# Decode attention with a gMLP branch: two heads interleaved over the partitions, 64 positions each

## The chip, the cores and the metric

The kernel runs on one core of one Trainium2 chip. The metric is the device time of one launch in microseconds (us), the median of several runs. A second source of numbers is one profiled execution of the same program, with a record of every instruction and every transfer.

## What is computed

One token `x` of 576 numbers is normalised to `xn`. Two branches read `xn`, and their results are added to `x`:

```python
# A: attention of 32 query heads over 16 key/value heads, head size 128,
#    over the last W = 4096 positions of the caches
q = (xn @ wq).reshape(32, 128)
k, v = k_cache[:, -4096:], v_cache[:, -4096:]      # each is used by two query heads
p = softmax(q @ k.T * 128 ** -0.5)
A = (p @ v).reshape(4096) @ wo                     # 4096 -> 576
# B: gMLP on one token
z = gelu(xn @ w_in)                                # 576 -> 4608
B = (z[:2304] * (w_sp * layernorm(z[2304:]) + b_sp)) @ w_out
out = x + A + B
```

All inputs and the output are bf16. Keys and values of one head are 1 MB each, so 32 MB of the 51 MB that are read are keys and values.

## The kernel before

**Loads.** All large inputs come through one queue, SP's, in a fixed order: `wq` in two pieces, the keys of the head pairs 0 and 1, `w_in` in three pieces, then in turn the keys of pair m and the values of pair m - 2 up to the last pair (7), the values of pairs 6 and 7, `w_out`, and `wo` in four pieces of 16, 10, 4 and 2 rows per partition. The pairs' loads are called k0 to k7 and v0 to v7 below. Each load fills one of seven slots of 20.7 KB per partition (pool `ring`); a load waits on SP until the slot it takes over has been read by its last user. `load_kv` puts position `32 p + t` of either head on partition p: two stretches of 8 KB per partition and load.

**Scores.** The loop over the 16 heads j works in groups of four (`GK = 4`, group g, place o = 0 to 3 in it). `t_head(j)` turns a head's keys with two 32x32 block transposes on VectorE (each 128x1024, as float32 pairs of bf16) into a tile `kT`; three such tiles exist. `s_head(j)` runs eight matmuls of 8 output rows and 512 columns: four accumulate (`be`) for either half `hf` of the positions. The result of head i of the group lies in rows 32 i to 32 i + 7 of the PSUM tile `S[g % 2]`, so a head uses one 32-column strip of the array. In a strip's eight rows, four rows `a` stand for four quarters of the partitions and two for the two query heads.

**Softmax of a group.** `sm_a(g)` takes the row maximum, lets `spread` exchange it between rows (two 32x32 transposes, a reduction, a copy), and ScalarE computes one exp over 128x1024 with the row sums into `lx`. `sm_b(g)` transposes the result `p` once (128x1024 bf16) into `pt`, runs `spread` again for the sums, takes the reciprocal `rs`, and ScalarE copies 16 pieces of 32x32 (as float32) from `pt` into `PT`, four per head.

**Values.** `pv(g)` runs 32 matmuls of 512 columns: 8 blocks `tb` of four positions, and in each block four heads i on four strips. `yb(g)` multiplies `ops` by `rs` and a mask (`om`), sums (`on`), and brings the result with 8 small matmuls into the columns of `Y`.

**Order.** The order of the instructions on each engine is the order in which the program writes them (`manual_schedule`). For head j of group g it is: `t_head(j)`; `sm_a(g - 1)` at o = 0 or `sm_b(g - 1)` at o = 1; `s_head(j)`; `yb(g - 2)` at o = 0; `pv(g - 1)` at o = 3. The gMLP's 162 matmuls (`z_mms`) come after head 3, its pointwise part (`z_rest`) after head 5 and `z_norm` after head 6. Behind the loop stand

```python
sm_a(3); sm_b(3); yb(2); pv(3); out_hv(0); out_hv(1); yb(3); out_hv(2)
for t, wv in wo_sb: out_mms(Y, t, wv, False, t == 31)
```

where `out_mms` runs four matmuls of 144 columns on four strips. The 128 matmuls of `wo` need all of `Y`, so also `yb(3)`. The heads' transposes are called t(0) to t(15) below, the score matmuls S(0) to S(15), and pv(g), exp(g), pt(g), om(g), Y(g) belong to group g.

Of the kernel before, what the change touches and what calls it, by code (L numbers as in the profile page):

```python
# [8 lines left out]
FP32 = mybir.dt.float32  # L9
BF16 = mybir.dt.bfloat16  # L10
ALU = mybir.AluOpType
ACT = mybir.ActivationFunctionType
AXX = mybir.AxisListType.X
# [3 lines left out]
HKV = 16  # L17
DH = 128
SK = 65536
W = 4096  # L20
F = 4608
FH = 2304
NT = W // 128
TB = 8
NB = NT // TB
GK = 4
NG = HKV // GK
NR = 98
NF = FH // 128
CW = D // 4  # L30
EPS = 1e-5
SCALE = DH ** -0.5
GELU_C = 0.7978845608028654
RING = 7
NS = 9
SLOT = NF * D
# [3 lines left out]
def kernel(  # L40
# [14 lines left out]
    nc = tc.nc  # L55
    P = nc.NUM_PARTITIONS

    const = ctx.enter_context(tc.tile_pool(name="const", bufs=1))
    work = ctx.enter_context(tc.tile_pool(name="work", bufs=2))
    ring = ctx.enter_context(tc.tile_pool(name="ring", bufs=RING))  # L60
    ktpool = ctx.enter_context(tc.tile_pool(name="ktpool", bufs=3))
    ps_s = ctx.enter_context(tc.tile_pool(name="ps_s", bufs=1, space=bass.MemoryType.PSUM))
    ps_o = ctx.enter_context(tc.tile_pool(name="ps_o", bufs=1, space=bass.MemoryType.PSUM))
    ps_m = ctx.enter_context(tc.tile_pool(name="ps_m", bufs=1, space=bass.MemoryType.PSUM))
    ps_a = ctx.enter_context(tc.tile_pool(name="ps_a", bufs=1, space=bass.MemoryType.PSUM))

    ctx.enter_context(tc.manual_schedule())

# [3 lines left out]
    def ring_tile(name, rows, width):  # L72
        t = ring.tile([P, SLOT], BF16, name=name, tag="ring")
        return t[:, 0:rows * width].rearrange("p (s c) -> p s c", c=width)
# [6 lines left out]
        return [(lo + s, v[:, s, :]) for s in range(n)]  # L81

    def load_kv(src, m, name):
        v = ring_tile(f"{name}{m}", 2, NT * DH)
        nc.sync.dma_start(v, src[0, 2 * m:2 * m + 2, SK - W:SK, :].rearrange("h (p t) d -> p h (t d)", p=P))
        return {2 * m + h: v[:, h, :].rearrange("p (t d) -> p t d", d=DH) for h in range(2)}

    def load_n(src, per, lo, n, name):
        v = ring_tile(f"{name}{lo}", n, D)
# [3 lines left out]
    K, V = {}, {}  # L93
    wq_sb = load_halves(A_wq, 0, 5, "wq") + load_halves(A_wq, 5, 4, "wq")
    for m in range(2):
        K.update(load_kv(A_k_cache, m, "k"))
    win_sb = sum((load_halves(B_w_in, lo, 3, "win") for lo in (0, 3, 6)), [])
    for m in range(2, HKV // 2):
        K.update(load_kv(A_k_cache, m, "k"))
        V.update(load_kv(A_v_cache, m - 2, "v"))  # L100
    for m in range(HKV // 2 - 2, HKV // 2):
        V.update(load_kv(A_v_cache, m, "v"))
    wout_sb = load_n(B_w_out, NF, 0, NF, "wout")
    wo_sb = []
    for n in (16, 10, 4, 2):
# [14 lines left out]
    ident = const.tile([P, P], BF16, name="ident")  # L120
# [18 lines left out]
    mask4 = const.tile([P, 4], FP32, name="mask4")  # L139
    nc.vector.reduce_sum(mask4[:], ident[:].rearrange("p (a x) -> p a x", a=4), axis=AXX)  # L140

    idv = ident[:].rearrange("p (i c h) -> p i c h", i=4, h=2)[:, :, 0:4, :]
    cm = const.tile([P, 4], FP32, name="cm")
    nc.vector.tensor_reduce(out=cm[:], in_=idv.rearrange("p i c h -> p c i h"), op=ALU.add,
                            axis=mybir.AxisListType.XY)
    dmask = const.tile([P, 4, DH], FP32, name="dmask")
    nc.gpsimd.tensor_copy(dmask[:], cm[:].unsqueeze(2).to_broadcast([P, 4, DH]))
    ihm = const.tile([P, 4, 2], FP32, name="ihm")
    nc.vector.reduce_sum(ihm[:], idv.rearrange("p i c h -> p i h c"), axis=AXX)

    sel = const.tile([P, 4, 32], FP32, name="sel")
    nc.gpsimd.memset(sel[:], 0.0)
    selv = sel[:].rearrange("p q (i h e) -> p q i h e", i=4, h=2)
    for dq in range(4):
        nc.gpsimd.tensor_copy(selv[:, dq, :, :, dq], ihm[:])
    S = []
    for n in range(2):
        t = ps_s.tile([P, 2, 512], FP32, name=f"S{n}")
        nc.vector.memset(t[:], 0.0)
        S.append(t)  # L160
    ops = ps_o.tile([P, 512], FP32, name="ops")
    nc.vector.memset(ops[:], 0.0)

    mx = const.tile([P, 32], FP32, name="mx")
    nc.gpsimd.memset(mx[:], 0.0)
    lx = const.tile([P, 32], FP32, name="lx")
    nc.gpsimd.memset(lx[:], 1.0)
    mb = const.tile([P, 32], FP32, name="mb")
    nc.gpsimd.memset(mb[:], 0.0)
    lb = const.tile([P, 32], FP32, name="lb")  # L170
    nc.gpsimd.memset(lb[:], 1.0)


    nc.tensor.matmul(ps_x[:, 0:NS], lhsT=rmat[:], rhs=x64[:], start=True, stop=True)  # L174
# [6 lines left out]
        out=junk[:], in0=x_col[:], in1=x_col[:], scale=1.0, scalar=0.0,  # L181
# [23 lines left out]
    for s, wv in wq_sb:  # L205
        for g in range(4):
            nc.tensor.matmul(  # L207
                qps[32 * g:32 * g + 2, :], lhsT=XT[:, s, :], rhs=wv[:, 512 * g:512 * (g + 1)],
                start=(s == 0), stop=(s == NS - 1), tile_position=(0, 32 * g),
# [12 lines left out]
    for k in range(4):  # L222
        for be in range(4):
            nc.tensor.matmul(
                qps2[:, k, be, :].rearrange("p (r g) -> p r g", r=2),
                lhsT=q_rep[0:NR, 2 * k + be // 2, be % 2].rearrange("p a d -> p (a d)"),
# [12 lines left out]
    KT = {}  # L239
    st = {}  # L240

    def t_head(j):
        kT = ktpool.tile([P, NT, 2, 32, 2], BF16, name=f"kT{j}", tag="kT")
        src = K[j].rearrange("p t d -> p (t d)").bitcast(FP32)
        dst = kT[:].rearrange("p t b k e -> p (t b k e)").bitcast(FP32)
        for hf in range(2):
            nc.vector.transpose(dst[:, 1024 * hf:1024 * (hf + 1)], src[:, 1024 * hf:1024 * (hf + 1)])  # L247
        KT[j] = kT

    def s_head(j):  # L250
        g, i = divmod(j, GK)
        kv = KT.pop(j)[:].rearrange("p t b k e -> p b e t k")
        for hf in range(2):
            for be in range(4):
                nc.tensor.matmul(  # L255
                    S[g % 2][32 * i:32 * i + 8, hf, :],
                    lhsT=Qb[:, j, be].rearrange("p a h -> p (a h)"),
                    rhs=kv[:, be // 2, be % 2, 16 * hf:16 * hf + 16, :],
                    start=(be == 0), stop=(be == 3), tile_position=(0, 32 * i),
                )  # L260

    def spread(col, buf, g, op, name):

        tr = work.tile([P, 32], FP32, name=f"{name}t{g}", tag=f"{name}t")
        nc.vector.transpose(tr[:], col[:])  # L265
        rd = work.tile([P, 2], FP32, name=f"{name}r{g}", tag=f"{name}r")
        nc.vector.tensor_reduce(out=rd[:], in_=tr[:, 0:8].rearrange("p (c h) -> p h c", h=2), op=op, axis=AXX)
        nc.vector.tensor_copy(buf[:, 0:8].rearrange("p (c h) -> p c h", h=2),
                              rd[:].unsqueeze(1).to_broadcast([P, 4, 2]))
        bk = work.tile([P, 32], FP32, name=f"{name}b{g}", tag=f"{name}b")  # L270
        nc.vector.transpose(bk[:], buf[:])  # L271
        return bk

    def sm_a(g):
        s = S[g % 2]
        nc.vector.tensor_reduce(out=mx[:, 0:1], in_=s[:], op=ALU.max, axis=mybir.AxisListType.XY)  # L276
        bk = spread(mx, mb, g, ALU.max, "m")
        nm = work.tile([P, 1], FP32, name=f"nm{g}", tag="nm")
        nc.vector.tensor_scalar_mul(nm[:], bk[:, 0:1], -SCALE)  # L279
        p = work.tile([P, 1024], BF16, name=f"p{g}", tag="p")  # L280
        nc.scalar.activation(p[:], s[:].rearrange("p a n -> p (a n)"), ACT.Exp, bias=nm[:, 0:1], scale=SCALE,  # L281
                             accum_out=lx[:, 0:1])
        st[g] = {"p": p}

    def sm_b(g):
        d = st[g]
        pt = work.tile([P, NT, 32], BF16, name=f"pt{g}", tag="pt")
        nc.vector.transpose(pt[:].rearrange("p t x -> p (t x)"), d["p"][:])  # L288
        lbk = spread(lx, lb, g, ALU.add, "l")
        rs = work.tile([P, 1], FP32, name=f"rs{g}", tag="rs")  # L290
        nc.vector.reciprocal(rs[:], lbk[:, 0:1])
        PT = work.tile([P, GK, NT, 2], BF16, name=f"PT{g}", tag="PT")
        pt4 = pt[:].rearrange("p t x -> p (t x)").bitcast(FP32).rearrange("p (t x) -> p t x", x=16)
        PT4 = PT[:].rearrange("p i t h -> p (i t h)").bitcast(FP32).rearrange("p (i t) -> p i t", i=GK)
        for i in range(GK):
            for a in range(4):
                nc.scalar.copy(PT4[32 * a:32 * a + 32, i, :], pt4[32 * i:32 * i + 32, :, a])  # L297
        d["PT"] = PT
        d["rs"] = rs

    def pv(g):
        d = st[g]
        for tb in range(NT // 4):
            for i in range(GK):
                nc.tensor.matmul(  # L305
                    ops[32 * i:32 * i + 8, :],
                    lhsT=d["PT"][:, i, 4 * tb:4 * tb + 4, :].rearrange("p t h -> p (t h)"),
                    rhs=V[GK * g + i][:, 4 * tb:4 * tb + 4, :],
                    start=(tb == 0), stop=(tb == NT // 4 - 1), tile_position=(0, 32 * i),
                )  # L310

    def yb(g):
# [64 lines left out]
        nc.vector.tensor_mul(hv[:], G[:, 0], zn[:])  # L377
        return hv

    for j in range(HKV):  # L380
        t_head(j)
        g, o = divmod(j, GK)
        if g > 0 and o == 0:
            sm_a(g - 1)
        if g > 0 and o == 1:
            sm_b(g - 1)
        s_head(j)
        if j == GK - 1:
            zps = z_mms()
        if j == GK + 1:  # L390
            G, sz = z_rest(zps)
            out_t = ps_a.tile([P, CW], FP32, name="out_t", tag="a")
            nc.vector.memset(out_t[:], 0.0)
        if j == GK + 2:
            hv = z_norm(G, sz)
        if g > 1 and o == 0:
            yb(g - 2)
        if g > 0 and o == 3:
            pv(g - 1)
# [58 lines left out]
```

## Time and profile before

| | before |
|---|---|
| median of 3 runs | 128.6 us (128.56 to 128.67) |
| the profiled execution: device time, span of its instructions | 128.68 us, 126.9 us |
| mean granted TensorE clock | 0.781 |
| busy: PE, VectorE (DVE), ScalarE (ACT), GpSimd (POOL) | 70.5, 74.1, 22.9, 3.6 us |
| read from memory | 50.96 MB, 402 GB/s over the span |
| transfers: packets of SP's queue, share of 16 engines' time | 5800, 95.2% |

Each line of groups names the source line, engine, operation, output and inputs, shapes and count, then the busy time and the mean duration of one instruction, then the engine's idle time just before it and what ended it. Matmuls are pipelined: a group's mean duration is a latency, and its rate is read from the times at which its matmuls start. "PEclk" is the granted TensorE clock, 1.00 being full speed.

### The profile page before, as it was taken

The page shows a single profiled execution, that of the slowest core. Times are in us where ns is not written, and L with a number is a line of the kernel's source. Part 1 is how long each engine was busy: PE and PEld are TensorE (multiplying, and loading weights), DVE is VectorE, ACT ScalarE, POOL GpSimd, SP SyncE. Part 2 cuts the span into 40 slices and gives each one's busy share as a digit, 9 for nine tenths or more (in the row PEclk, how much of TensorE's full clock was granted, in tenths as well). Part 3 has the DMA queues.
Part 4 walks back from the last instruction along what each step waited for, and adds up shares of the span by engine and source line. Part 5 has one row for each costly group of instructions (what it writes and reads, how often), then busy time and mean ns, then how long its engine had stood idle before and what let it go on. Part 6 is the DMA issues. An engine that isn't in the chain of part 4 may idle for free.

```text
span 126.9 us, 1775 instructions
## 1 busy us (share of the span) xinstructions
PE 70.5 (56%) x708; PEld 32.5 (26%) x708; DVE 74.1 (58%) x157; ACT 22.9 (18%) x76; POOL 3.6 (3%) x19
## 2 busy tenths in 40 slices
PE   0002831399999796008359456991579901862460
PEld 0002301132699621002113111231113301222350
DVE  6704145999000499455399799997999557050000
ACT  0300011000000003930000308303074039200000
POOL 3401000000000000000100000000000000000000
PEclk9999996579985559955868976999555996589755
DMA  4999999999999999999999999999999999999940
GB/s 136 433 409 429 408 429 434 444 436 418 427 413 431 418 426 429 421 431 434 421 436 423 424 436 423 429 424 421 429 431 423 431 452 442 427 418 413 415 171 0
DMA packets 5899, 51.06 MB, mean 402 GB/s; under 512 B 516, under 2 KB 516, under 8 KB 772
## 3 DMA queue, kind: packets, MB, share of 16 engines
q1 hardware_dynamic: 5800, 50.96, 95.2%
q8 instruction: 5, 0.08, 0.2%
q10 hardware_dynamic: 92, 0.00, 0.0%
q14 instruction: 2, 0.02, 0.0%
HBM read 50.96 MB, written 0.00 MB: 402 GB/s over the span
## 4 chain that ended last, share of the span: by engine, by line
issue 41%; DVE 27%; DMA 25%; PE 3%; POOLq 0%; POOL 0%
DMA wo<-in_A_wo_dram 18%; DVE kT L247 16%; DMA x<-in_A_x_dram 7%; PE out_t L403 2%; DVE mx L276 2%; DVE pt L288 2%; DVE on L319 2%; DVE om L315 1%; PE yps L322 1%; PE ps_x L184 0%; POOLq L453 0%; POOL mv L190 0%; DVE mt L265 0%; DVE lb L271 0%; DVE mb L271 0%
## 5 line engine op out<-in xcount | busy, mean ns | idle before, releaser
L255 PE MATMUL S<-kT,Qb 128*8 128x512 bf16 x128 | 40.5, 484 | 21.8 <-DVE kT L247 21.0
L247 DVE STREAM_TRANSPOSE kT<-k 128x1024 f32<-128x1024 f32 x32 | 37.0, 1211 | 10.8 <-DMA k<-in_A_k_cache_dram 10.8
L255 PEld LDWEIGHTS <-Qb 128*8 128x8 bf16 x128 | 11.7, 98 | 46.7 <-issue 38.5
L297 ACT COPY PT<-pt 32x32 f32<-32x32 f32 x64 | 15.4, 241 | 13.7 <-DVE pt L288 12.9
L281 ACT ACTIVATE p<-S,nm 128x1024 bf16<-128x1024 f32 x4 | 4.5, 1113 | 54.8 <-DVE nm L279 54.8
L305 PE MATMUL ops<-v,PT 128*8 128x512 bf16 x128 | 13.3, 453 | 0.4 <-ACT PT L297 0.4
L334 PEld LDWEIGHTS <-win 128*128 128x128 bf16 x162 | 10.1, 164 | 0.4 <-issue 0.4
L334 PE MATMUL zps<-XT,win 128*128 128x2 bf16 x162 | 10.2, 202 | 0.0
L322 PE MATMUL yps<-on,sel 128*32 128x32 f32 x32 | 2.1, 220 | 10.8 <-DVE on L319 10.8
L403 PE MATMUL out_t<-wo,Y 128*1 128x144 bf16 x128 | 3.7, 276 | 5.2 <-DMA wo<-in_A_wo_dram 5.2
L276 DVE TENSOR_REDUCE mx<-S 128x1 f32<-128x1024 f32 x4 | 4.8, 1204 | 1.6 <-PE S L255 1.6
L425 DVE TENSOR_TENSOR res<-out_t,x 97x144 bf16<-97x144 f32 x1 | 0.3, 308 | 9.1 <-PE out_t L403 9.1
L288 DVE STREAM_TRANSPOSE pt<-p 128x1024 bf16<-128x1024 bf16 x4 | 4.8, 1210 | 1.4 <-ACT p L281 1.4
L305 PEld LDWEIGHTS <-PT 128*8 128x8 bf16 x128 | 4.0, 91 | 5.8 <-issue 2.0
L174 PE MATMUL ps_x<-x,rmat 64*128 64x9 bf16 x1 | 0.2, 163 | 9.5 <-DMA x<-in_A_x_dram 9.5
L315 DVE SCALAR_TENSOR_TENSOR om<-ops,rs,dmask 128x512 f32<-128x512 f32 x4 | 3.0, 742 | 4.2 <-PE ops L305 4.2
L322 PEld LDWEIGHTS yps<-on,sel 128*32 128x32 f32 x32 | 1.7, 132 | 12.5 <-DVE on L319 10.4
L403 PEld LDWEIGHTS <-Y 128*1 128x1 bf16 x128 | 2.9, 97 | 6.0 <-issue 5.9
L207 PE MATMUL qps<-wq,XT 128*2 128x512 bf16 x36 | 3.8, 603 | 0.8 <-DVE XT L198 0.8
L319 DVE TENSOR_REDUCE on<-om 128x128 f32<-128x512 f32 x4 | 4.1, 1023 | 0.1
L218 DVE CAST q_rep<-qps 128x512 bf16<-128x512 f32 x2 | 1.4, 692 | 4.4 <-PE qps L207 3.7
L216 ACT CAST q_rep<-qps 128x512 bf16<-128x512 f32 x2 | 1.2, 585 | 14.2 <-DVE q_rep L218 14.2
(88 smaller groups left out, 35.0 us busy)
## 6 DMA issues: line engine op xcount, KB each, us to landing
k<-in_A_k_cache_dram SPq DMA_DIRECT2D x8, 2048.0 KB, 24.9
v<-in_A_v_cache_dram SPq DMA_DIRECT2D x8, 2048.0 KB, 21.7
win<-in_B_w_in_dram SPq DMA_DIRECT2D x3, 1728.0 KB, 20.6
wout<-in_B_w_out_dram SPq DMA_DIRECT2D x1, 2592.0 KB, 27.4
wq<-in_A_wq_dram SPq DMA_DIRECT2D x1, 2560.0 KB, 8.8
wo<-in_A_wo_dram SPq DMA_DIRECT2D x1, 2304.0 KB
wq<-in_A_wq_dram SPq DMA_DIRECT2D x1, 2048.0 KB, 13.0
wo<-in_A_wo_dram SPq DMA_DIRECT2D x1, 1440.0 KB
```

Of the source, the lines that this page charges most:

```text
L247: nc.vector.transpose(dst[:, 1024 * hf:1024 * (hf + 1)], src[:, 1024 * hf:1024 * (hf + 1)])
L255: nc.tensor.matmul(S[g % 2][32 * i:32 * i + 8, hf, :], lhsT=Qb[:, j, be].rearrange("p a h -> p (a h)"), rhs=kv[:, be // 2, be % 2, 16 * hf ...
L276: nc.vector.tensor_reduce(out=mx[:, 0:1], in_=s[:], op=ALU.max, axis=mybir.AxisListType.XY)
L281: nc.scalar.activation(p[:], s[:].rearrange("p a n -> p (a n)"), ACT.Exp, bias=nm[:, 0:1], scale=SCALE, accum_out=lx[:, 0:1])
L288: nc.vector.transpose(pt[:].rearrange("p t x -> p (t x)"), d["p"][:])
L297: nc.scalar.copy(PT4[32 * a:32 * a + 32, i, :], pt4[32 * i:32 * i + 32, :, a])
L305: nc.tensor.matmul(ops[32 * i:32 * i + 8, :], lhsT=d["PT"][:, i, 4 * tb:4 * tb + 4, :].rearrange("p t h -> p (t h)"), rhs=V[GK * g + i][:, ...
L315: nc.vector.scalar_tensor_tensor(out=om[:].rearrange("p c d -> p (c d)"), in0=ops[:], scalar=d["rs"][:, 0:1], in1=dmask[:].rearrange("p c ...
L319: nc.vector.reduce_sum(on[:], om[:].rearrange("p c d -> p d c"), axis=AXX)
L322: nc.tensor.matmul(yps[32 * g:32 * g + 32, :], lhsT=sel[:, dq, :], rhs=on[:, 32 * dq:32 * dq + 32], start=(dq == 0), stop=(dq == 3), tile_ ...
L334: nc.tensor.matmul(zps[:, :, t], lhsT=wt[:, t, :], rhs=XT[:, s, :], start=(s == 0 and t == 0), stop=(s == NS - 1 and t == NF - 1), skip_gr ...
L403: nc.tensor.matmul(out_t[32 * n:32 * n + 1, :], lhsT=lhs[:, col:col + 1], rhs=wv[:, CW * n:CW * (n + 1)], start=first, stop=last, tile_pos ...
```

## The change

Half-heads take the place of heads. A pair's keys (and values) now lie with head 0 on the even and head 1 on the odd partitions, 64 consecutive positions of 16 KB on each. One step of the loop (`t_half`, `s_half`) handles half of the 64 positions for both heads of a pair; there are still 16 steps, and four steps make a group of two pairs.

- `load_kv` asks for one stretch of 16 KB per partition. The order, the sizes and the slots of the loads stay.
- `t_half` transposes as much as `t_head` did. `s_half` runs eight matmuls, four for head 0 on strip `pr`, then four for head 1 on strip `2 + pr` (`pr` is the pair in the group). Each reads all of `kT`, every fourth bf16 of it instead of every second.
- exp is done by two instructions of 64 rows, one per head `hd`, into every second column of a tile `pz` of 128x2048 that GpSimd has set to zero at the start.
- `pt` becomes 128x2048: two transposes instead of one.
- The sums are spread by one float32 matmul with a constant matrix `lsum` (result `lps`), a maximum with 0.5 and a reciprocal, instead of `spread`.
- The 16 copies into `PT` are 32x64 instead of 32x32.
- `pv` still runs 32 matmuls of 512 columns, now with 16 output rows, in 16 blocks of two: only the strips 0 and 1 are used.
- The order of the tile pools in memory is changed (`lead`, then `ring` come first), and the constants `cm`, `sel` follow the new order of rows.

```diff
     def load_kv(src, m, name):
-        v = ring_tile(f"{name}{m}", 2, NT * DH)
-        nc.sync.dma_start(v, src[0, 2 * m:2 * m + 2, SK - W:SK, :].rearrange("h (p t) d -> p h (t d)", p=P))
+        t = ring.tile([P, SLOT], BF16, name=f"{name}{m}", tag="ring")
+        v = t[:, 0:TP * DH]
+        nc.sync.dma_start(v, src[0, 2 * m:2 * m + 2, SK - W:SK, :].rearrange("h (r t) d -> r h (t d)", t=TP))
...
+    lsum = const.tile([P, 4, 8, 2, 2], FP32, name="lsum")
+    nc.gpsimd.memset(lsum[:], 0.0)
...
+    for n in range(2):
+        t = const.tile([P, TP, 16, 2], BF16, name=f"pz{n}")
+        nc.gpsimd.memset(t[:], 0.0)
+        pz.append(t)
...
-    def s_head(j):
-        kv = KT.pop(j)[:].rearrange("p t b k e -> p b e t k")
-        for hf in range(2):
+    def s_half(m, hf):
+        kv = KT.pop((m, hf))[:].rearrange("p t b r x e -> p b e x t r")
+        for hd in range(2):
+            i = 2 * hd + pr
             for be in range(4):
                 nc.tensor.matmul(
                     S[g % 2][32 * i:32 * i + 8, hf, :],
-                    lhsT=Qb[:, j, be].rearrange("p a h -> p (a h)"),
-                    rhs=kv[:, be // 2, be % 2, 16 * hf:16 * hf + 16, :],
+                    lhsT=Qb[:, 2 * m + hd, be].rearrange("p a h -> p (a h)"),
+                    rhs=kv[:, be // 2, be % 2, hd],
...
-        nc.scalar.activation(p[:], s[:].rearrange("p a n -> p (a n)"), ACT.Exp, bias=nm[:, 0:1], scale=SCALE,
-                             accum_out=lx[:, 0:1])
+        for hd in range(2):
+            lo, hi = 64 * hd, 64 * hd + 64
+            nc.scalar.activation(p[lo:hi, :, :, hd], s[lo:hi].rearrange("p a (t r) -> p (a t) r", r=16), ACT.Exp,
+                                 bias=nm[lo:hi, 0:1], scale=SCALE, accum_out=lx[lo:hi, 0:1])
...
-        nc.vector.transpose(pt[:].rearrange("p t x -> p (t x)"), d["p"][:])
-        lbk = spread(lx, lb, g, ALU.add, "l")
-        nc.vector.reciprocal(rs[:], lbk[:, 0:1])
+        for n in range(2):
+            nc.vector.transpose(dst[:, 1024 * n:1024 * (n + 1)], src[:, 1024 * n:1024 * (n + 1)])
+        nc.tensor.matmul(lps[:], lhsT=lsum[:].rearrange("p q c x h -> p (q c x h)"), rhs=lx[:], start=True, stop=True)
+        nc.vector.tensor_scalar_max(rs[:], lps[:], 0.5)
+        nc.vector.reciprocal(rs[:], rs[:])
...
-                nc.scalar.copy(PT4[32 * a:32 * a + 32, i, :], pt4[32 * i:32 * i + 32, :, a])
+                nc.scalar.copy(PT4[32 * a:32 * a + 32, i % 2, i // 2, :], pt4[32 * i:32 * i + 32, :, a])
...
-        for tb in range(NT // 4):
-            for i in range(GK):
+        for tb in range(TP // 4):
+            for pr in range(2):
                 nc.tensor.matmul(
-                    ops[32 * i:32 * i + 8, :],
+                    ops[32 * pr:32 * pr + 16, :],
...
-                    start=(tb == 0), stop=(tb == NT // 4 - 1), tile_position=(0, 32 * i),
+                    start=(tb == 0), stop=(tb == TP // 4 - 1), tile_position=(0, 32 * pr),
```

## Prediction

> **What bounds the kernel now.** I read the page's slices first, then the chain, a table by stretches of time, SP's queue, and last the timeline of the end.
>
> ```profile
> PEclk9999996579985559955868976999555996589755
> DMA  4999999999999999999999999999999999999940
> GB/s 136 433 409 429 408 429 434 444 436 418 427 413 431 418 426 429 421 431 434 421 436 423 424 436 423 429 424 421 429 431 423 431 452 442 427 418 413 415 171 0
> ```
>
> The transfers are full from the second slice (3.2 us) to the thirty-eighth (120.6 us). The chain says what waits for them:
>
> ```profile
> 93.55 4.53 DVE kT L247 x4
> 98.08 0.02 issue
> 98.10 23.38 DMA wo<-in_A_wo_dram
> 121.48 0.04 issue
> 121.52 1.37 PE out_t L403 x30
> ```
>
> The last pieces of `wo` are issued about when t(15) frees a slot (98.1) and land at 121.5, behind 23 us of queued data. So today's end is: last byte at 121.5, then 64 matmuls of `wo`, then the output. The stretches answer whether a longer stretch per partition moves bytes faster:
>
> ```profile
> 24.00:36.00 12.00, 11.40 (x80) 5.57 (x80) 8.03 (x8) 0.00 (x0) 0.00 (x0) 0.88 1.00 428
> 44.00:104.00 60.00, 36.52 (x210) 11.61 (x209) 47.98 (x91) 16.61 (x57) 0.55 (x1) 0.77 1.01 427
> 106.00:118.00 12.00, 6.36 (x120) 2.85 (x121) 3.38 (x6) 2.56 (x11) 0.00 (x0) 0.74 1.00 425
> ```
>
> The last number is GB/s. The first line is mostly `w_in` (13.8 KB per partition and load), the second keys and values (8 KB), the third `w_out` and `wo` (20.7 and 18 KB). All three are 425 to 428 at a full DMA share (last but one). Nothing is to be had from 16 KB.
>
> What remains is how far the computation trails the last byte, so I read the end:
>
> ```profile
> 102.13 1.11 ACT L281 ACTIVATE p<-S,nm 128x1024 bf16<-128x1024 f32 x1 [5.42 <-DVE nm L279]
> 103.36 1.25 DVE L288 STREAM_TRANSPOSE pt<-p 128x1024 bf16<-128x1024 bf16 x1 [1.35 <-ACT p L281]
> 104.64 4.06 ACT L297 COPY PT<-pt 32x32 f32<-32x32 f32 x16 [1.31 <-DVE pt L288]
> 108.76 3.57 PE L305 MATMUL ops<-v,PT 128*8 128x512 bf16 x29 [0.39 <-ACT PT L297]
> 112.36 0.75 DVE L315 SCALAR_TENSOR_TENSOR om<-ops,rs,dmask 128x512 f32<-128x512 f32 x1 [4.20 <-PE ops L305]
> 114.71 0.20 DVE L326 CAST Y<-yps 32x32 bf16<-32x32 f32 x1 [0.53 <-PE yps L322]
> 118.10 1.29 PE L403 MATMUL out_t<-wo,Y 128*1 128x144 bf16 x64 [3.06 <-DMA wo<-in_A_wo_dram]
> 121.52 2.46 PE L403 MATMUL out_t<-wo,Y 128*1 128x144 bf16 x64 [2.12 <-DMA wo<-in_A_wo_dram]
> ```
>
> The eight lines are one dependent chain, exp to `wo`. `Y` is complete at 114.9; the first `wo` matmul waits for data until 118.1. The computation has only 3.2 us of slack, and the change makes nearly every link longer. The last 64 matmuls took 2.46 us where the first 64 took 1.29: the clock was at 0.50 after 119.0, and at 1.00 from 112.1 to 119.0.
>
> **Part by part.** *Transfers.* Bytes, order and slots stay; packets fall by 2048 (16 loads x 128). I cost that at nothing by the three equal rates, and let k2 land at 42.85 (where t(4) waited for it) and `wo` at 121.5. The Trainium skill ("DMA: Bandwidth & Descriptors", section "Latency and other measured facts") speaks against the layout: copies whose neighbouring partitions lie a large power of two apart ran at half rate or less, and neighbours are now 16 MB apart. If that held, 32 MB would take some 75 us longer. The row is nearer: before, each partition already took 8 KB from each of two places 16 MB apart, at 427 GB/s. I keep 0 to +5% (+4 us) for the changed pattern.
>
> *SP's waits.* A later release could starve the queue. The closest call is k6, issued at 66.1 when t(7) ended: the 14 loads before it hold 31.0 MB, which at 427 GB/s from 3 us on last until 75.6, so 9.5 us of cover. The next, v4 and k7, wait for pv(0) and have the same cover plus k6's 4.9 us, less the 3.7 us by which they come later. The delays below are 1.4 to 3 us there, so starvation costs nothing.
>
> *Start.* GpSimd gets two memsets of 2048 columns, a small one and four copies ahead of the power at 11.70, on which `xn` waits. Memsets of 32 and 128 float32 columns took 124 and 199 ns, 0.78 ns a column, so 1.7 us each; with 0.2 and 0.6 for the rest GpSimd is done at 4.6 + 4.2 = 8.8. Cover 2.9 us. At twice that price 0.5 us would show, and the wait for k2 hides it.
>
> *Per group.* ACTIVATE and its read of the sum take 1.2 us together; two in a row make exp 1.2 us longer. `pt` grows by one transpose, +1.13. VectorE loses the second `spread` (76.51 to 77.29: 0.78) and gains a maximum, 0.17: net +0.52 with the transpose. A copy of 32 columns comes every 0.253 us; exp's slope ((1113 - 233) ns over 988 columns) adds 0.03 for 32 more: 16 x 0.281 = 4.5 us, +0.45 (bounds: none, or 1.0). The `lps` matmul (0.4 to 0.6 us, as L364 and L184) waits on PE for exp with S of the next step behind it; that step's transposes end 0.3 us before to 3 us after exp, so its cost is under 1 us in one group.
>
> *pv.* A strip's matmul starts every 0.427 us at clock 0.5 and every 0.215 at 1.0 (S rows: 65.38, 65.80; five per 1.07 us at 28). Four strips ran beside each other (eight rounds, 29 matmuls in 3.57 us), so 8 rounds of four become 16 rounds of two: 3.4 us warm, 6.8 cold, against 1.7 and 3.4.
>
> *S.* Before, the first four matmuls started after the first of two transposes; now all wait for both. But they lie on two strips, and in the trace pv's matmuls on the strips 0 to 2 ran beside S(7) on strip 3, about four matmuls ahead. So S ends 1.05 us (warm) to 1.9 (cold) after its transposes if the two overlap, as before (1.6 for S(15)); 1.9 to 3.6 if they don't. I take the overlap.
>
> *The sum,* before to after. exp(0) ends 49.95, `pt` 52.25, the copies 54.9 to 56.8; the gelu's exp behind them drags VectorE's t(6) from 56.4 to 58.3. S(6), with both transposes and a cold clock, ends 62.55 (61.1), and `z_norm` behind it delays t(7) from 63.7 to 65.1. t(8) ends 69.75 (68.3). om(0) would start at 72.05, but pv(0), started at 67.9 partly cold, ends between 72.5 and 73.6: I take a wait of 1.0, which holds t(9) behind it: 75.55 (73.1). pv(1) starts at 85.3 warm and ends 89, before om(1): no wait (2.6 if cold). With 0.52 twice, t(15) ends 101.6 (98.1), and the maximum starts 103.2 (99.7). Then exp ends 108.1 (103.3), `pt` 110.35 (104.5), the copies 114.95 (108.7). PE has been nearly idle since 106, so pv(3) starts cold; before, the clock rose 4.6 us after its first matmul (107.5 to 112.1): 4.6 us for 10.8 rounds, 5.2 rounds x 0.215, 0.2 to drain, 5.9 us: 120.85 (112.3). `om` to `Y` as before 2.55: 123.4. All of `wo` has landed by then, PE is warm from pv(3): 128 matmuls x 0.020 = 2.6: 126.0, against 123.98. So **+2.0 us**: span 128.9, device time 130.7 with the 1.8 us around the span; the profiled run lay 0.08 above the median: **130.6**.
>
> By the clock rule of the Trainium skill ("TensorE: Matmul & The Clock Gate", Part 1) about 3.4 us of sustained matmuls are enough to raise it, counted in free-running windows. That would make pv(3) 5.3 us and the time 130.0; the trace's 4.6 us fits a window that began later.
>
> **Rivals.** *Faster: the tail's slack swallows it.* `Y` at 121.1 or earlier ends before 123.7, since PE stays warm and 64 matmuls after 121.5 take 1.3 us instead of 2.46. That needs 2.3 us less than my sum: no wait of om(0) (1.0), pv(3) at 5.3 (0.6), copies as before (0.45), S(15) warm (0.5). Together 2.55: 128.0; the floor is 121.5 + 1.3 = 122.8: 127.4. Against it: every one has to fall well.
>
> *S doesn't overlap* (two strips share the read of `kT`, or reading every fourth bf16 is slow). Then +0.85 to 1.7 at S(6), at pv(0) and at S(15): 132.5 to 134.5. Nothing in the trace reads so; reading every second ran at full rate.
>
> *Transfers slower by 5%* on keys and values: `wo` lands at 125.3 and steps that wait for keys move too: 131 to 134.
>
> *The transfers alone decide*, and the tail is covered: within 0.2% of now; it needs `Y` within a narrow band.
>
> **How the numbers follow.** My sum 0.50 (129.2 to 132), S without overlap 0.18, slower transfers 0.07, a cold pv(1) or `wo` (+2.3) on top 0.02, faster 0.18, no change 0.05. 0.2% (0.26 us) is about what a measurement tells from no change. Slower holds 0.77. The range 128.1 to 134.5 leaves out most of the faster case and the worst of the S case.
>
> **What would show it.** Right: GB/s stays near 427; exp pairs 2.4 us, copies near 0.28 us apart, pv at two per round; `Y` complete at 122 to 125 and no DMA wait ahead of the last `wo` matmuls. Wrong: a `wo` wait at 121.5 still in the chain (then the faster rival), S matmuls of one step starting one by one (the S rival), GB/s under 415, or t(9) not later than 74.

## The result and the profile after

The changed kernel takes 133.45 us (median of five runs from 132.66 to 134.31; a sixth, at 134.97, counts as a slow one and is left out) against 128.58 before. The ratio is 1.0377, with a 95% interval of [1.0335, 1.0419], or 4.9 us slower. The forecast was 130.6 us, 2.0 slower. The profiled execution took 133.33 us with a span of 131.5 at a mean granted clock of 0.766; the one before took 128.68 and 126.9.

The slices of the page, each 3.29 us long:

```profile
PEclk9999995559955586865777986869855599555999
DMA  4999999999999999999999999999999999997000
GB/s 143 449 395 438 419 443 423 421 446 420 438 428 424 438 416 433 428 423 448 423 428 438 423 438 424 443 419 428 436 428 438 425 441 422 424 428 318 18 5 0
```

The DMA row now ends three slices before the span does. The transfers run out between 121 and 122.5 us, about 0.5 us earlier than before, and the end belongs to the computation: the chain of waits no longer holds a transfer of `wo`. The middle of the table by stretches (busy times per engine, granted clock, DMA share, GB/s) says that no transfer starved or slowed on the way:

```profile
44.00:104.00 60.00, 30.11 (x182) 9.35 (x183) 46.82 (x77) 23.13 (x61) 0.55 (x1) 0.73 1.01 431
106.00:118.00 12.00, 4.76 (x37) 2.02 (x34) 6.33 (x13) 7.18 (x19) 0.00 (x0) 0.74 1.00 430
```

431 and 430 GB/s stand where 427 and 425 stood. The timeline of the end (start, duration, engine, line and operation, in brackets the idle time before and what ended it) has the same links as before, and those from exp to `pv` are longer:

```profile
105.76 1.23 DVE L298 TENSOR_REDUCE mx<-S 128x1 f32<-128x1024 f32 x1 [2.09 <-PE S L277]
...
108.18 1.39 ACT L305 ACTIVATE pz<-S,nm 64x1024 bf16<-64x1024 f32 x1 [4.45 <-DVE nm L301]
...
109.65 1.39 ACT L305 ACTIVATE pz<-S,nm 64x1024 bf16<-64x1024 f32 x1
...
111.11 2.37 DVE L315 STREAM_TRANSPOSE pt<-pz 128x1024 bf16<-128x1024 bf16 x2 [3.05 <-ACT pz L305]
...
113.52 4.89 ACT L327 COPY PT<-pt 32x64 f32<-32x64 f32 x16 [2.44 <-DVE rs L320]
...
118.47 4.92 PE L335 MATMUL ops<-v,PT 128*16 128x512 bf16 x28 [0.64 <-ACT PT L327]
...
123.44 0.38 PE L335 MATMUL ops<-v,PT 128*16 128x512 bf16 x1
...
123.86 0.75 DVE L345 SCALAR_TENSOR_TENSOR om<-ops,rs,dmask 128x512 f32<-128x512 f32 x1 [7.51 <-PE ops L335]
...
126.19 0.20 DVE L356 CAST Y<-yps 32x32 bf16<-32x32 f32 x1 [0.53 <-PE yps L352]
126.44 2.17 PE L433 MATMUL out_t<-wo,Y 128*1 128x144 bf16 x128
```

From the first exp to the last copy it is 10.23 us (108.18 to 118.41) where it was 6.57 (102.13 to 108.70); then `pv` adds 5.4 us (to 123.82) where it took 3.6. `Y` is complete at 126.39, 11.5 us later than before. All 128 `wo` matmuls then run without a wait.

On the way there `om` waits for `pv` in two earlier groups, which it did not before (the timeline around them):

```profile
74.22 0.75 DVE L345 SCALAR_TENSOR_TENSOR om<-ops,rs,dmask 128x512 f32<-128x512 f32 x1 [1.26 <-PE ops L335]
...
91.58 0.75 DVE L345 SCALAR_TENSOR_TENSOR om<-ops,rs,dmask 128x512 f32<-128x512 f32 x1 [1.09 <-PE ops L335]
```

The same two lines before the change, without a wait:

```profile
70.54 0.74 DVE L315 SCALAR_TENSOR_TENSOR om<-ops,rs,dmask 128x512 f32<-128x512 f32 x1
...
86.39 0.74 DVE L315 SCALAR_TENSOR_TENSOR om<-ops,rs,dmask 128x512 f32<-128x512 f32 x1
```

VectorE runs in the order of the program, so each wait delays the key transposes behind it.

### The profile page after: what moved, and what is told of

Its sections match the earlier page's. It is cut to its first block, busy times and chain, and to the rows that moved or that the text cites. A ratio compares the mean times of both kernels' runs of the same rounds, so it can differ in the third digit from the quotient of the medians.

```text
span 131.5 us, 1799 instructions
## 1 busy us (share of the span) xinstructions
PE 68.9 (52%) x716; PEld 31.2 (24%) x716; DVE 76.7 (58%) x150; ACT 33.2 (25%) x84; POOL 7.7 (6%) x25
## 3 DMA queue, kind: packets, MB, share of 16 engines
q1 hardware_dynamic: 3752, 50.96, 91.1%
## 4 chain that ended last, share of the span: by engine, by line
issue 41%; DVE 26%; PE 18%; DMA 7%; ACT 6%; POOLq 0%; POOL 0%; ACTq 0%
DVE kT L268 12%; PE ops L335 9%; DMA x<-in_A_x_dram 7%; PE S L277 5%; DVE pt L315 5%; ACT PT L327 3%; DVE on L349 2%; ACT pz L305 2%; PE out_t L433 2%; DVE om L345 2%; PE yps L352 1%; DVE mx L298 1%; PE ps_x L204 0%; POOLq L483 0%; POOL mv L210 0%
## 5 line engine op out<-in xcount | busy, mean ns | idle before, releaser
L277 PE MATMUL S<-kT,Qb 128*8 128x512 bf16 x128 | 32.3, 635 | 30.3 <-DVE kT L268 30.3
L305 ACT ACTIVATE pz<-S,nm 64x1024 bf16<-64x1024 f32 x8 | 11.2, 1402 | 51.9 <-DVE nm L301 51.8
L335 PE MATMUL ops<-v,PT 128*16 128x512 bf16 x128 | 22.3, 436 | 1.8 <-ACT PT L327 1.8
L327 ACT COPY PT<-pt 32x64 f32<-32x64 f32 x64 | 18.9, 296 | 16.2 <-DVE rs L320 10.2
L277 PEld LDWEIGHTS <-Qb 128*8 128x8 bf16 x128 | 6.3, 95 | 48.2 <-issue 45.4
L315 DVE STREAM_TRANSPOSE pt<-pz 128x1024 bf16<-128x1024 bf16 x8 | 9.4, 1210 | 3.8 <-ACT pz L305 3.8
L335 PEld LDWEIGHTS <-PT 128*16 128x16 bf16 x128 | 7.1, 95 | 12.9 <-issue 4.8
L317 PE MATMUL lps<-lx,lsum 128*128 128x1 f32 x8 | 1.7, 278 | 5.2 <-ACT pz L305 5.2
L400 POOL TENSOR_TENSOR mz<-mz,mhalf 128x1 f32<-128x1 f32 x1 | 0.6, 552 | 52.4 <-DVE mz L399 52.4
L176 POOL MEMSET pz<- 128x2048 bf16 x2 | 3.5, 1804 | 0.0
```

Source lines behind the costliest of these rows:

```text
L176: nc.gpsimd.memset(t[:], 0.0)
L277: nc.tensor.matmul(S[g % 2][32 * i:32 * i + 8, hf, :], lhsT=Qb[:, 2 * m + hd, be].rearrange("p a h -> p (a h)"), rhs=kv[:, be // 2, be % 2 ...
L305: nc.scalar.activation(p[lo:hi, :, :, hd], s[lo:hi].rearrange("p a (t r) -> p (a t) r", r=16), ACT.Exp, bias=nm[lo:hi, 0:1], scale=SCALE, ...
L315: nc.vector.transpose(dst[:, 1024 * n:1024 * (n + 1)], src[:, 1024 * n:1024 * (n + 1)])
L327: nc.scalar.copy(PT4[32 * a:32 * a + 32, i % 2, i // 2, :], pt4[32 * i:32 * i + 32, :, a])
L335: nc.tensor.matmul(ops[32 * pr:32 * pr + 16, :], lhsT=d["PT"][:, pr, 4 * tb:4 * tb + 4].rearrange("p t x h -> p (t x h)"), rhs=V[2 * g + p ...
```

## The experiments

The theory after the result: the transfers lost nothing, and the 4.9 us are the computation's: `pv` on two strips (twice as waits on VectorE, once at the end), exp with its strided output, the transpose and the copies, the scores. The rivals: slower transfers, and one part that explains everything. Each run was timed beside the kernel before, which took 128.5 to 128.73 us in these sessions; the changed kernel was timed only for the result, so differences from it are between sessions. Below, the array is called warm when it runs at the prediction's full rate (a matmul of 512 columns every 0.215 us on a strip) and cold at half of it (0.427), and an unread matmul is one whose result nobody reads, put in only to keep the array busy.

### The layout of the loads alone

The kernel before, with only the new pattern of addresses in `load_kv`:

```diff
-  nc.sync.dma_start(v, src[0, 2*m:2*m+2, SK-W:SK, :].rearrange("h (p t) d -> p h (t d)", p=P))
+  nc.sync.dma_start(v.rearrange("p h n -> p (h n)"),
+      src[0, 2*m:2*m+2, SK-W:SK, :].rearrange("h (r t) d -> r h (t d)", t=2*NT))
```

> The kernel before with only the loads of keys and values changed: head 0 on the even, head 1 on the odd partitions, 16 KB each (the computation then takes other positions and heads together than it should; its work is the same). Theory (the loss is all in the computation's chain at the end, the layout costs and brings nothing): 128.2 to 128.8 us, GB/s of the middle stretch 425 to 432, the last wo matmuls start at 121.0 to 121.6. Rival (the layout slows the transfers, or starts the end later): over 129.5 us. Rival (fewer packets land the data earlier): under 128.0 us.

Measured: 128.1 us, ratio 0.9954 [0.994, 0.9967]: 0.6 us faster than before. That ends the rival of slower transfers, and it misses my own expectation by 0.1 us: the layout is a small gain and not nothing. Its table by stretches:

```profile
44.00:104.00 60.00, 39.16 (x210) 12.11 (x208) 47.18 (x90) 16.61 (x57) 0.55 (x1) 0.68 1.01 431
```

To see which of its two properties brings it, the larger pieces came from one head (the second head of a pair then gets positions of the first):

```diff
+  nc.sync.dma_start(v.rearrange("p h n -> p (h n)"),
+      src[0, 2*m, SK-2*W:SK, :].rearrange("(p t) d -> p (t d)", p=P))
```

> The kernel before with pieces of 16 KB per partition that come from one head only: the keys and values are not interleaved by heads, only the size of a piece is that of the change. The new layout of the loads alone took 128.1 us (0.9954 of before). If that gain of 0.6 us is the larger piece, this takes 128.0 to 128.3 us and the packets of the queue fall from 5800 to about 3750; if it is the interleaving or the order in which the heads come, it takes 128.5 to 128.8 us. A larger piece also arrives later than its first half would, which could cost up to 0.5 us at the start.

Measured: 127.97 us, ratio 0.9948 [0.9934, 0.9961], and 3752 packets where there were 5800. The table by stretches of this run:

```profile
44.00:104.00 60.00, 36.72 (x210) 11.54 (x209) 47.82 (x91) 16.60 (x57) 0.55 (x1) 0.77 1.01 431
```

It is 431 GB/s in the same stretch, without any interleaving. What the two runs share is the size of the piece, 16 KB against 8 KB per partition, so this brings the gain. It also sets the level that the changed kernel could reach if its computation were hidden: 128.0 us.

### What the transfers leave as a floor

The prediction's faster rival took 121.5 + 1.3 us as the earliest end, with a warm array. The kernel before with unread matmuls (`warm`) ahead of and between the `wo` matmuls tests it:

```diff
+  warm(14)
   for t, wv in wo_sb:
+      if t == 16: warm(9)
       out_mms(Y, t, wv, False, t == 31)
```

> The kernel before with 14 unread matmuls of 512 columns ahead of the first and 9 ahead of the second half of the wo matmuls, so that PE doesn't fall to clock 0.5 while it waits for data. The prediction's floor (the clock alone makes the last 64 matmuls 2.46 instead of 1.29 us): 127.3 to 127.9. Theory after reading the traces again (the last two pieces of wo land at about 122.9 and 123.5, and the matmuls follow them one by one): 128.3 to 128.8, no difference.

Measured: 128.51 us, ratio 0.9991 [0.998, 1.0001]: no difference. Its timeline of the last `wo` matmuls:

```profile
121.33 0.80 PE L412 MATMUL out_t<-wo,Y 128*1 128x144 bf16 x40 [0.32 <-DMA wo<-in_A_wo_dram]
122.69 0.42 PE L412 MATMUL out_t<-wo,Y 128*1 128x144 bf16 x16 [0.57 <-DMA wo<-in_A_wo_dram]
123.47 0.30 PE L412 MATMUL out_t<-wo,Y 128*1 128x144 bf16 x8 [0.35 <-DMA wo<-in_A_wo_dram]
```

Even a warm array waits three times, and the last time until 123.47. What I had read as one landing at 121.5 and 2.46 us of cold matmuls was three pieces that land one after another. So with the loads of the kernel before the earliest end is 123.8 (123.47 + 0.30), 1.0 us later than the 122.8 that the prediction took, and a warm array at the end was worth nothing.

### `pv` on four strips

The changed kernel, with even blocks on strips 0 and 1 and odd blocks on strips 2 and 3; the constants that sum the strips follow:

```diff
+  st4 = pr + 2 * (tb % 2)
-  ops[32 * pr:32 * pr + 16, :],
+  ops[32 * st4:32 * st4 + 16, :],
-  start=(tb == 0), stop=(tb == TP // 4 - 1), tile_position=(0, 32 * pr),
+  start=(tb < 2), stop=(tb >= TP // 4 - 2), tile_position=(0, 32 * st4),
```

> The changed kernel with pv on four strips again: even blocks of positions on the strips 0 and 1, odd ones on 2 and 3, added up by the small matmuls that bring the result into Y (their constant matrix and that of the sums repeat the rows). 8 rounds of four instead of 16 of two. Theory (pv on two strips stretches the chain at the end and holds om of groups 0 and 1): pv(3) lasts 3.4 to 3.8 us instead of 6.6, om's waits for pv (1.3, 1.1 and 7.5 us) fall to 0, 0 and about 4.5; time 128.3 to 130.0 us. Rival (the half-step order of transposes and scores sets the pace, pv hides behind it): at least 132.5 us. Rival (it is the transfers): no change, 133.4.

Measured: 129.22 us, ratio 1.0048 [1.0032, 1.0065]; 4.2 us of the 4.9 are gone. The timeline of its end:

```profile
103.30 1.22 DVE L301 TENSOR_REDUCE mx<-S 128x1 f32<-128x1024 f32 x1 [2.10 <-PE S L280]
...
111.05 4.90 ACT L330 COPY PT<-pt 32x64 f32<-32x64 f32 x16 [2.44 <-DVE rs L323]
...
116.00 3.37 PE L339 MATMUL ops<-v,PT 128*16 128x512 bf16 x31 [0.64 <-ACT PT L330]
...
119.42 0.75 DVE L349 SCALAR_TENSOR_TENSOR om<-ops,rs,dmask 128x512 f32<-128x512 f32 x1 [5.55 <-PE ops L339]
...
122.01 2.17 PE L437 MATMUL out_t<-wo,Y 128*1 128x144 bf16 x128
```

Two things add up. The last `pv` ends 3.4 us behind the copies, near the 3.6 before the change, and not 5.4: 2.0 us. And the two waits of `om` are gone, which brings the last maximum from 105.76 to 103.30: 2.5 us against the 2.35 that the waits had taken. Together that is 4.5 us; the two profiled executions differ by 4.3 (133.33 and 128.99). So `pv` on half of the strips is worth most of the loss by itself, though the runs below show that other parts are worth a good deal too and overlap with it.

### A warm array ahead of the last `pv`

The changed kernel with 9 unread matmuls before and 4 behind `yb(2)`:

```diff
   sm_b(g)
+  warm(9)
   yb(g - 1)
+  warm(4)
   pv(g)
```

> The changed kernel with 13 matmuls of 508 columns that nobody reads on PE ahead of pv(3), in the time in which PE waits for exp, the transposes and the copies. Theory (pv(3) ran at clock 0.5 since PE had been idle: 16 rounds of 0.427): the clock is at 1.00 by the middle of pv(3) at the latest, pv(3) lasts 3.5 to 5 us instead of 6.6, time 130.3 to 132.0. Rival (two strips with 16 rows are slow at either clock, as the scores were 0.45 us a round at 0.5 and at 1.0): pv(3) stays at 6 us or more, 133.2 or more.

Measured: 131.95 us, ratio 1.0264 [1.0237, 1.029], 1.5 less than the changed kernel, near the upper end of what was expected. The timeline:

```profile
113.39 2.70 PE L264 MATMUL wps<-dummy,XT 128*2 128x508 bf16 x6 [1.97 <-DVE rs L328]
...
118.29 3.29 PE L343 MATMUL ops<-v,PT 128*16 128x512 bf16 x28
```

The main part of `pv` takes 3.29 us where it took 4.92: its cold start is worth about 1.6 us. The 13 matmuls need 5 us (113.39 to 118.35) and just fit ahead of the last copy (118.24).

### Exp into a row

The changed kernel with exp writing 1024 columns in a row:

```diff
-  nc.scalar.activation(p[lo:hi, :, :, hd], ...
+  nc.scalar.activation(p[lo:hi].rearrange("p t r x -> p (t r x)")[:, 1024*hd:1024*hd+1024], ...
```

> The changed kernel with exp's two instructions of 64 rows writing 1024 columns in a row instead of every second column (the rest of the work is the same, its input isn't what it should be). Theory (writing every second column makes one exp 1.40 us instead of 1.11): the mean falls to 1.11 to 1.15, exp(0) and exp(3) end 0.5 to 0.6 earlier, time 132.3 to 132.9. Rival (64 rows, or two instructions in a row, are slow in themselves): the mean stays at 1.40 and the time at 133.4.

The group of the changed kernel (busy us, mean ns of one, idle before):

```profile
L305 ACT ACTIVATE pz<-S,nm 64x1024 bf16<-64x1024 f32 x8 | 11.2, 1402 | 51.9 <-DVE nm L301 51.8
```

The same group with the row:

```profile
L305 ACT ACTIVATE pz<-S,nm 64x1024 bf16<-64x1024 f32 x8 | 8.9, 1109 | 51.7 <-DVE nm L301 51.6
```

The operation and its size are the same, only the spacing of the output differs: 1402 ns against 1109, so the stride alone costs 0.29 us an instruction. The time fell to 131.49 us, ratio 1.0231 [1.0198, 1.0264], 2.0 less than the changed kernel and more than the theory gave. The timeline of its end:

```profile
107.81 1.11 ACT L305 ACTIVATE pz<-S,nm 64x1024 bf16<-64x1024 f32 x1 [4.45 <-DVE nm L301]
...
109.04 2.47 DVE L315 STREAM_TRANSPOSE pt<-pz 128x1024 bf16<-128x1024 bf16 x2 [1.35 <-ACT pz L305]
...
111.54 4.89 ACT L327 COPY PT<-pt 32x64 f32<-32x64 f32 x16 [1.31 <-DVE rs L320]
...
116.49 5.91 PE L335 MATMUL ops<-v,PT 128*16 128x512 bf16 x28 [0.64 <-ACT PT L327]
```

The rest is an overlap that the strided layout forbids: with each head in its own half, the first transpose starts when the first exp is done (109.04). From the start of exp to the first copy it is 3.73 us (107.81 to 111.54) instead of 5.34, and the last copy is done 2.0 us earlier (116.43). This profiled execution took 132.43 us, 0.9 more than the median: its last `pv` took 6.4 us behind the copies and not 5.4, since the clock rose later (see *The end* below).

### Half of the transpose and of the copies

```diff
-  for n in range(2):
-      nc.vector.transpose(dst[:, 1024*n:1024*(n+1)], src[:, 1024*n:1024*(n+1)])
+  nc.vector.transpose(dst[:, 0:1024], src[:, 0:1024])
-  nc.scalar.copy(PT4[32*a:32*a+32, i % 2, i // 2, :], pt4[32*i:32*i+32, :, a])
+  nc.scalar.copy(PT4[32*a:32*a+32, i % 2, i // 2, 0:NT], pt4[32*i:32*i+32, 0:NT, a])
```

> The changed kernel with half of the work between exp and pv: only the first 1024 of the 2048 columns are transposed, and the 16 copies move 32x32 instead of 32x64 (half of the probabilities stay zero, so half of the positions are left out of the result). Theory (everything between exp and pv lies on the chain at the end): copies 4.05 instead of 4.9 us, one transpose less, 1.2 us: the chain of group 3 is 2.0 us shorter, and group 0's delay of t(6) is 2 us shorter as well; time 129.8 to 131.6. Rival (only the copies and transposes of one group count, the others are hidden): 131.3 to 131.6 and no earlier t(6). Rival (pv's 6.6 us hides them): 133.4.

(`PT` is set to zero once at the start, so that the half which isn't copied is zero.)

Measured: 128.1 us, ratio 0.9988 [0.9959, 1.0017], with ten runs in two groups (six from 127.75 to 128.18, four from 129.0 to 129.35). That is 5.3 us less than the changed kernel, where the theory gave 1.8 to 3.6. The timeline of its profiled execution (129.33 us, one of the four):

```profile
73.41 0.75 DVE L349 SCALAR_TENSOR_TENSOR om<-ops,rs,dmask 128x512 f32<-128x512 f32 x1 [2.53 <-PE ops L339]
...
89.65 0.75 DVE L349 SCALAR_TENSOR_TENSOR om<-ops,rs,dmask 128x512 f32<-128x512 f32 x1 [1.12 <-PE ops L339]
...
102.72 1.23 DVE L303 TENSOR_REDUCE mx<-S 128x1 f32<-128x1024 f32 x1 [2.10 <-PE S L282]
...
109.35 4.04 ACT L331 COPY PTc<-pt 32x32 f32<-32x32 f32 x16 [1.31 <-DVE rs L324]
...
113.44 5.93 PE L339 MATMUL ops<-v,PTc 128*16 128x512 bf16 x28 [0.42 <-ACT PTc L331]
```

The last copy is done at 113.39, 5.0 us earlier than in the changed kernel: 2.0 of it lie between exp and the last copy, as the theory had it, and 3.0 lie ahead of the last maximum. Of the 2.1 us by which t(6) starts earlier (56.91 instead of 59.00, behind the gelu's exp, which waits for the copies on ScalarE) only 0.8 are left at t(9), since `om` now waits 2.53 us for `pv`. The other 2.2 are what the theory had left out: one transpose less, 1.1 us each, on VectorE's path in groups 1 and 2.

These four experiments take away 4.2, 1.5, 2.0 and 5.3 us, 13 in all, of a loss of 4.9 (5.5 against the 128.0 of the transfers). They can't be summed: four strips and the warm array shorten the same last `pv`, what the copies give back in group 0 turns for the most part into a longer wait of `om`, and gains end at the level of the transfers, which half of the copies reaches.

### How the scores are read

The prediction took a score round, two matmuls beside each other on two strips, at 0.215 us on a warm array. The changed kernel shows 0.45 everywhere. The first test was the changed kernel with scores that read every second bf16:

```diff
-  kv = KT.pop((m, hf))[:].rearrange("p t b r x e -> p b e x t r")
+  kv = KT.pop((m, hf))[:].rearrange("p t b (x r) y e -> p b e x t (r y)", x=2)
```

> The changed kernel with the score matmuls reading every second bf16 of kT, as before, and not every fourth (they read half of what they should for one head and the other's for the other; the count and the size are the same). Rival of the prediction (reading every fourth bf16 limits two strips to 0.45 us a round at full clock): at clock 1.0 a round of two falls to 0.22 us and S ends 1.1 us after its transposes; time 132.4 to 133.2. Theory (two strips that read one tile cost 0.45 us a round whatever the step): rounds stay at 0.45 us at either clock, time 133.0 to 134.0.

Measured: 134.82 us, ratio 1.0456 [1.0417, 1.0495], not faster, against both theories. Its median lies 1.4 above the changed kernel's, but the runs of the two overlap (133.36 to 134.96 here, 132.66 to 134.31 there). Two of its score steps, and the stretch from 25 to 31 us:

```profile
27.77 1.88 PE L277 MATMUL S<-kT,Qb 128*8 128x512 bf16 x8 [0.37 <-DVE kT L268]
...
32.27 1.04 PE L277 MATMUL S<-kT,Qb 128*8 128x512 bf16 x8 [0.46 <-DVE kT L268]
...
25.00:31.00 6.00, 4.74 (x22) 1.29 (x23) 6.00 (x6) 0.00 (x0) 0.00 (x0) 1.00 1.02 438
```

The rounds of the steps from 25.5 us on were 0.43 us apart although the granted clock stands at 1.00 there, and the step at 32.27 ran at 0.22. So the question was open whether 0.45 is the price of the read or of a cold array. Two runs with unread matmuls around the first four score steps settle it:

```diff
   def s_half(m, hf):
+      if m == 0 and hf == 0: warm(20)
       ...
+      if m < 2: warm(6)
```

> The changed kernel with 20 unread matmuls of 508 columns ahead of the first score step and 6 behind each of the first four, so that TensorE does not rest between 20 and 34 us; nothing else is added, and the whole result is computed. Question: does reading every fourth bf16 cost time of its own, or did a round of two take 0.45 us because the array was cold whatever the clock row said. Theory (cold array): the score rounds of the steps behind the unread matmuls start 0.21 to 0.24 us apart, eight matmuls in about 1.05 us. Rival (the read costs): 0.45 us apart although the unread matmuls beside them start every 0.21 us. The time itself says little: 133 to 136 us.

> The same with the score matmuls reading every second bf16 instead of every fourth (the scores then belong to other positions than the values). Both theories: rounds 0.21 to 0.24 us apart behind the unread matmuls; it is the measure for the run beside it. If they are 0.43 apart here too, two strips share something else.

The second score step and the unread matmuls behind it, every fourth bf16:

```profile
29.67 2.01 PE L287 MATMUL S<-kT,Qb 128*8 128x512 bf16 x8
...
31.50 0.83 PE L264 MATMUL wps<-dummy,XT 128*2 128x508 bf16 x3
```

and every second:

```profile
29.23 1.03 PE L287 MATMUL S<-kT,Qb 128*8 128x512 bf16 x8
...
30.10 0.80 PE L264 MATMUL wps<-dummy,XT 128*2 128x508 bf16 x3
```

The unread matmuls run at full rate in both (three in 0.83 and 0.80 us), so the array is warm in both, and eight score matmuls take 2.01 us against 1.03. The read costs: a round of two is 0.45 us when every fourth bf16 is read and 0.22 when every second is. So the cold-array theory has fallen for the changed kernel, while the 0.43 with every second bf16 was a cold array, whatever the granted clock says there; why the two disagree stays open. Why undoing the slow read alone didn't make the kernel faster is known in part. In its trace `om` waited 2.25 and 1.55 us for `pv` instead of 1.26 and 1.09, and the last maximum started 0.95 us later (106.71). The granted clock between 62 and 80 us was 0.69 instead of 0.78; that this comes of the shorter scores is argued, not shown. The times of the two runs, 134.81 and 134.94 us (one run each), carry the added matmuls.

### A version that beats both

`pv` on four strips and the 13 unread matmuls together:

> The changed kernel with both: pv on four strips and 13 unread matmuls ahead of pv(3), so that the clock is up. The result is that of the reference. Theory (the computation's end falls back under the transfers' end, which the load-only kernel shows at 123.0 us): pv(3) lasts 1.9 to 2.6 us, Y is complete by 120.5, the last wo matmuls wait for data again; time 127.7 to 128.4, so faster than before by 0.2 to 0.7%. Rival (the chain at the end still decides): 128.6 to 129.2.

Measured: 127.99 us over 12 runs, ratio 0.9955 [0.9939, 0.9971]: 0.6 us faster than before and 5.5 faster than the changed kernel. This is the level that the new loads reach alone (128.0). The moved pools, the sums by `lsum`, the strided exp, the longer copies and the slow read of the scores are all still in this kernel, so at the median none of them costs anything that the transfers don't hide.

Two of the 12 runs lie at 129.0, the others from 127.8 to 128.4. The profiled execution is one of the two (129.05):

```profile
73.88 0.75 DVE L357 SCALAR_TENSOR_TENSOR om<-ops,rs,dmask 128x512 f32<-128x512 f32 x1 [0.77 <-PE ops L347]
...
122.15 2.17 PE L445 MATMUL out_t<-wo,Y 128*1 128x144 bf16 x128
```

Here `om` of group 0 still waits 0.77 us, which it didn't in the run with four strips alone, and the `wo` matmuls run without a wait: in this execution the computation still sets the end. No execution of the other ten was profiled, so that the transfers set the end there follows from their time alone, and what splits the two groups, here and in the run with half of the copies, isn't shown.

## Why the prediction was right and wrong

The direction and the mechanism were right: the transfers kept their rate, the computation overtook them, no `wo` wait was left. The size was wrong: the forecast added 2.0 us, the measurement 4.9. What failed is the sum of the computation's chain, which came out 2.6 us too short: its signs gave exp pairs of 2.4 us and `Y` at 122 to 125, and the trace has 2.9 us and 126.4. By its own steps, in the profiled executions (the 92.1 of t(13) is worked out from the forecast's delays):

| | forecast | measured | late | added here |
|---|---|---|---|---|
| t(6) starts | 58.3 | 59.00 | 0.70 | 0.70 |
| t(7) starts | 65.1 | 66.16 | 1.06 | 0.36 |
| t(9) starts | 75.55 | 76.69 | 1.14 | 0.08 |
| t(13) starts | 92.1 | 94.14 | 2.04 | 0.90 |
| the last maximum starts | 103.2 | 105.76 | 2.56 | 0.52 |
| exp(3) is done | 108.1 | 111.08 | 2.98 | 0.42 |
| `pt`(3) is done | 110.35 | 113.48 | 3.13 | 0.15 |
| the copies are done | 114.95 | 118.41 | 3.46 | 0.33 |
| pv(3) is done | 120.85 | 123.82 | 2.97 | -0.49 |
| `Y` is complete | 123.4 | 126.39 | 2.99 | 0.02 |
| the last `wo` matmul ends | 126.0 | 128.61 | 2.61 | -0.38 |

The steps that failed are four terms of the sum that were too small; the two at the end were too large, which by luck took 0.9 us of the error back.

*Exp* ("two in a row make exp 1.2 us longer"): 1.70 longer in the last group (2.93 us from start to transpose, 1.23 before). The price was that of a contiguous write. No row showed a strided one, and I set no bound for it; that is the plainest fault. The contiguous run measured the stride at 0.29 us an instruction.

*The copies* ("16 x 0.281 = 4.5 us, +0.45 (bounds: none, or 1.0)"): 4.89, +0.83, inside the bounds and nearer to their upper end. With exp it makes nearly all of the 0.70 of the first row and most of the 0.90 from the maximum to the copies.

*om(1)* ("pv(1) starts at 85.3 warm and ends 89: no wait (2.6 if cold)"): it started at 86.1 and ended at 91.5. Its first rounds run 0.45 apart beside S(11), and its last ones between the matmuls of S(12). The wait of 1.09 moved all that followed. With `pv` on four strips it was gone.

*The scores* ("1.05 us (warm) to 1.9 (cold)"): 2.0 to 2.1 at either, since the read of every fourth bf16 sets it. By the trace it cost 0.5 at the last maximum, and part of the 0.36 at t(7); no run shows a gain from undoing it alone. The prediction had named the slow read as half of its second rival. The result lies in that rival's range (132.5 to 134.5), but not by its price: the two strips did overlap, and the price there was 0.85 to 1.7 us in three places.

*The end.* pv(3) took 5.4 us behind the last copy and not 5.9. By the clock rule of the Trainium skill ("TensorE: Matmul & The Clock Gate", Part 1), about 3.4 us of sustained matmuls, the prediction had worked out 5.3, and in this execution the clock did rise 3.5 us after the first of the 28 matmuls (118.47 to 122.0). But that is one draw: the same cold `pv` took 6.4, 6.4, 5.8, 5.6 and 5.8 us behind the last copy in the profiles of the runs with exp in a row, half of the copies, every second bf16 and the two with unread matmuls at the scores, and in the first two of them the clock rose only after 5.5 us. So the forecast's 5.9, from a row of 4.6 us, lies within what the runs show. The `wo` matmuls took 2.17 and not 2.6.

*The floor of the transfers.* "Nothing is to be had from 16 KB" was wrong by 0.6 us: rates within 1% were read as the same, but 1% of 118 us is 1.2 us, and a measurement here tells 0.26. In the changed kernel this gain is lost, since the end no longer waits for data. The faster rival's floor, 127.4, was not to be had either, as the warm run of the kernel before showed: the prediction had read three pieces of `wo` that land one after another as one.

*Right as they stood:* no starvation (k6 issued at 68.6, v4 and k7 at 74.0 and 74.6, the rate unbroken), GpSimd's two memsets (1.80 us each, done at 8.7, forecast 8.8), the first wait of `om` (1.26, forecast 1.0), S on two strips beside each other. The loads ahead of k6 are 15 and not 14; their 31.0 MB are right, and nothing hangs on the count.

## What to carry to other kernels

Where a change turns contiguous reads and writes into strided ones, the price of the contiguous row is only the lower bound: give each strided operand a range of its own, and expect the errors to add up where all of them lie on one chain. Count how many strips a matmul keeps busy before counting matmuls: the same 32 matmuls a group on two strips instead of four were worth 4.2 us here. And a queue on one engine turns every wait into a delay of all that follows, so a `pv` that is late in an early group is paid at the end: waits of 2.35 us in two groups moved the last maximum by 2.5.

## What the runs showed of the hardware

- ScalarE's exp over 1024 columns into every second bf16 column took 1402 ns, into a row 1109.
- A matmul that reads every fourth bf16 of its moving operand starts its rounds of two strips 0.45 us apart, every second 0.22, on an array that is warm in both.
- Pieces of 16 KB per partition instead of 8 KB moved 431 GB/s instead of 427, and brought 0.5% of the whole time (128.1 and 127.97 us in two layouts). Taking neighbouring partitions in turn from two places 16 MB apart cost nothing (431 GB/s); the pieces of each head follow one another in memory, so this says nothing of 128 places that far apart.
- The granted clock rose from 0.50 to 1.00 between 3.5 and 5.5 us after the first of the 28 matmuls of the last `pv`, in the executions of the changed kernel and its variants; so the same cold `pv` took from 5.4 to 6.4 us behind the last copy.
- The last pieces of a queue land one after another: the matmuls waited until 121.33, 122.69 and 123.47 us.
- The granted clock stood at 1.00 between 25 and 31 us while the score steps that read every second bf16, with gaps between them, ran at half rate (0.43 us a round); with unread matmuls in the gaps, the same matmuls ran at 0.22. The record of the clock alone does not say how fast a matmul runs.
